# A pair's products with v in one run, in the banks of its scores, for the last two batches

## The chip, the cores and the metric

The program runs on one core of a Trainium2 chip. The metric is the device time of one execution in microseconds. On the core, TensorE multiplies matrices (PE in the profile; PEld is its loading of weights), VectorE (DVE), ScalarE (ACT) and GpSimd (POOL) work on tiles, and SyncE (SP) issues the DMAs. TensorE writes its results to PSUM, which has 8 banks of 512 float32 words in each of 128 partitions; the tiles that the engines read lie in SBUF.

## The reference

Causal attention with a decay (4 batches, 8 heads, 576 positions, 64 wide), then a gated feed-forward layer (512 to 1536 to 512), then a second feed-forward layer of 8 experts (1024 wide) that are mixed by a balanced gate. All is float32.

```python
scores = scale * np.matmul(q, k.transpose(0, 1, 3, 2))
decay = cum[:, :, :, None] - cum[:, :, None, :]
scores = np.where(causal, -1000000000.0, scores + decay)
attn = np.exp(scores - np.max(scores, axis=-1, keepdims=True))
attn = attn / (np.sum(attn, axis=-1, keepdims=True) + 1e-09)
out = np.matmul(attn, v)
...
g = x @ w_gate
x = (g * (1.0 / (1.0 + np.exp(-g))) * (x @ w_val)) @ w_out      # 2304 tokens
...
for e in range(8):
    out += P[:, e:e + 1] * (np.maximum(x @ w1[e], 0.0) @ w2[e])
```

## The kernel before, in words

The work is laid out in stages. Attention of batch 0 runs alone; attention of batches 1, 2 and 3 runs beside the first feed-forward layer of batches 0, 1 and 2; then comes that layer for batch 3, and after it the experts, which take most of the time. `merge` emits the steps of two streams (attention and feed-forward) in proportion to fixed costs, and a scheduler of the framework then sets the order of each engine's instructions from the dependences and its own estimate of times. Every engine works its own list strictly in order, so the list can be read from the program, and a wait holds up all that stands behind it.

Attention takes two heads (a pair, `hp`) at a time, four pairs per batch. The 576 queries of a head are four blocks of 128 (`qi` 0 to 3) and a last one of 64 (both heads' last blocks share one tile). Per pair the steps are: `load`; `front_a` (scores of blocks 0 and 1); `back_a` (their exponentials, tiles `np`, turned by TensorE into PSUM, `ps_t`, copied to `pts[0]`, and multiplied with v: `pv(hp, 0)`); `front_b` and `scores_end` (scores of the other blocks); `back_b` (the same for blocks 2, 3 and the last into `pts[1]`, then `pv(hp, 1)`); `fold` (the products, tile `bt`, times the reciprocals of the row sums, `rb`, and split into a high and a low part, `xh` and `xl`, which the feed-forward layer of that batch reads).

Scores go to `ps_s` (two banks, one tile at a time in these stages), turned blocks to `ps_t` (two tiles of a bank), products with v to `ps_o` (one bank, one tile), and the feed-forward layer has `ps_m` (three banks: `pm` for the products with w_gate and w_val, `py` for those with w_out, `pl` for the gate's logits). Nearly all matmuls use the whole array, 128 columns of weights. The products with v do not: a head's v is 64 wide, so each takes one half of the array's columns (128x64 weights), and the two heads of a pair are sent in turns (`e` 1, then 0). `pv(hp, 0)` has 2 blocks of keys and `pv(hp, 1)` has 5, so 4 and 10 matmuls; they are float32, and the profile counts each as two. `behind(one)` asks the scheduler to keep a run's matmuls together.

Batches 2 and 3 (`MASKED`) differ from 0 and 1: their scores come from split operands (`qkw`), and the decay and the mask (`cb`, `cm`, `cd`, loaded by DMA and added to on GpSimd) are added by VectorE in `step` and not by TensorE. The change touches these two batches only.

The reciprocals of a pair's row sums take a way of their own: ScalarE and VectorE make `rc`, TensorE turns it (`ps_r`), VectorE copies it (`rt`), a DMA writes it to DRAM (`rd`), four DMAs read it back spread over the partitions (`rb`).

Of the kernel before, what the change touches and what calls it, by code (L numbers as in the profile page):

```python
# [8 lines left out]
F32 = mybir.dt.float32  # L9
# [24 lines left out]
def attention_two_ffns(ctx: ExitStack, tc: tile.TileContext, qkT, vt, f, wf, g2, w1, w2, out):  # L34
    nc = tc.nc
# [5 lines left out]
    P = 128  # L41
# [23 lines left out]
    ident = const.tile([P, P], F32, name="ident")  # L65
# [13 lines left out]
    for rows, c in ((slice(0, 64), 0), (slice(64, P), 64)):  # L79
        nc.vector.tensor_copy(out=maskd[rows], in_=maskf[rows, rows])  # L80
        nc.vector.tensor_reduce(
            out=picks[rows], in_=ident[rows, c:c + 3 * NG].rearrange("p (n j) -> p n j", j=3),
# [65 lines left out]
    last_pv = [None]  # L148
# [5 lines left out]
    MASKED = (2, 3)  # L154
# [59 lines left out]
    for e in range(2):  # L214
        spread_in = nc.sync.dma_start(
            out=spread[64 * e:64 * e + 3 * NG],
            in_=cumt[16 * e:16 * e + NG].rearrange("n j s -> (n j) s"))

    WA, WB = 256, 320
# [7 lines left out]
    pts = [ptp.tile([P, n, 2, w], F32, name=f"pt{n}") for n, w in ((2, WA), (5, WB))]  # L227
# [2 lines left out]
        nc.vector.memset(vss[i][0:64, 4], 0.0)  # L230

    def attn_unit(b, ps_s, ps_t, ps_o):
        heads = {}

        def load(hp):
            if hp == 0:
# [42 lines left out]
        def behind(ins):  # L279
            hold = ExitStack()  # L280
            if ins is not None:
                hold.enter_context(tc.issue_after(ins.ins))
                hold.enter_context(tc.high_priority(offset=SOON))
            return hold
# [125 lines left out]
        def turn(pt, n, k0):  # L410
            ps = ps_t.tile([P, 512], F32, tag="t", name="ps_t")
            for j in range(n):
                c = k0 + j * P
                nc.tensor.transpose(ps[:, j * P:(j + 1) * P], pt[:, c:c + P], ident)  # L414
            return ps[:, 0:n * P]

        def trans(hp, qi, e):
            n = qi + 1
            ps = turn(heads[hp][-1].pop((qi, e)), n, 0)
            c = qi % 2 * P  # L420
            copy = nc.vector.tensor_copy if qi in ONV else nc.scalar.copy
            copy(out=pts[qi // 2][:, 0:n, e, c:c + P], in_=ps.rearrange("p (j q) -> p j q", j=n))

        def trans_end(hp):
            pt = heads[hp][-1].pop(4)
            ps = turn(pt, 4, 0)
            nc.vector.tensor_copy(
                out=pts[1][:, 0:4, :, 256:WB], in_=ps.rearrange("p (j e q) -> p j e q", j=4, e=2))
            ps = turn(pt, 1, 448)
            nc.scalar.copy(out=pts[1][:, 4, :, 256:WB], in_=ps.rearrange("p (e q) -> p e q", e=2))  # L430

        def pv(hp, rng):
            vs, bt = heads[hp][4:6]
            w, t0 = ((WA, 0), (WB, 256))[rng]
            po = ps_o.tile([P, 512], F32, tag="o", name="ps_o")
            one, n = None, (2, 5)[rng]
            for j in range(n):
                c0 = max(0, j * P - t0)
                for e in (1, 0):
                    rows = HALF[e]  # L440
                    with behind(one):
                        one = nc.tensor.matmul(  # L442
                            out=po[rows, c0:w], lhsT=vs[:, j, rows], rhs=pts[rng][:, j, e, c0:w],
                            start=(j == 0), stop=(j == n - 1))
            last_pv[0] = one
            nc.scalar.copy(out=bt[:, t0:t0 + w], in_=po[:, 0:w])

        def fold(hp):
            bt = heads[hp][5]
# [18 lines left out]

        def back_a(hp):
            for qi in range(2):  # L470
                for e in range(2):
                    trans(hp, qi, e)
            pv(hp, 0)

        def front_b(hp):
            scores(hp, 2)
# [2 lines left out]
        def back_b(hp):  # L479
            for qi in range(2, 4):  # L480
                for e in range(2):
                    trans(hp, qi, e)
            trans_end(hp)
            pv(hp, 1)

        return [(c, lambda fn=fn, hp=hp: fn(hp)) for hp in range(H // 2) for c, fn in
                ((0.6, load), (1.6, front_a), (1.4, back_a), (2.4, front_b), (1.6, scores_end), (4.0, back_b), (0.3, fold))]


# [101 lines left out]
    with ExitStack() as hold:  # L591
        room = banks(hold, 2, 3)
        idle = room[1].tile([P, 512], F32, tag="t", name="idle")
        for _ in range(WARM):
            nc.tensor.matmul(out=idle[:, 0:P], lhsT=ident, rhs=ident, start=True, stop=True)
        for n, (_, fn) in enumerate(attn_unit(0, *room)):
            fn()
            for i in LOADS.get(n, ()):
                sts[i] = wload0(i, spread_in if i == 1 else last_qk[0])
            if n in ROWS:  # L600
                rows.append(last_step[0])
            if n in TURNS:
                w0.append(convert(len(w0)))
# [8 lines left out]
    ps_m = m_ctx.enter_context(pool("ps_m", 3, space=PSUM, reuse_waits="tile"))  # L612
    room = banks(at_ctx, 1, 2)
    merge(attn_unit(1, *room), moe_unit(0, convert, w0), lead=LA)
    merge(attn_unit(2, *room), moe_unit(1), lead=LB)
    merge(attn_unit(3, *room), moe_unit(2), lead=LC)
    at_ctx.close()
# [303 lines left out]
```

## Time and profile before

| What | Value |
|---|---|
| median of 3 runs | 2212.11 us (2211.51 to 2214.68) |
| the profiled execution's own time | 2213.49 us |
| its span, from the first to the last instruction | 2211.7 us |
| PE busy | 2174.7 us, 98% of the span |
| DVE busy | 1603.3 us, 72% |
| ACT busy | 780.1 us, 35% |
| POOL busy | 837.0 us, 38% |

The granted clock of TensorE is a share of full speed: 1.00 is its level of 2.4 GHz and 0.50 that of 1.2 GHz; 0.996 is the mean over the span. In a timeline, a row is a group of like instructions that follow each other, with the start of the first, the time from there to the end of the last, and their count at the end; a bracket behind it tells how long the engine had been idle before and what it waited for. Matmuls overlap, so the time that a group costs is not its own length but the distance from its start to the start of the next group. Attention of batches 2 and 3 falls between about 240 and 511 us.

### The profile page before, as it was taken

Reading aid. Unit: us, or ns where it says so; the run is one execution under the profiler, and the core shown is the slowest. Engines: PE = TensorE matmul, PEld = TensorE weight load, DVE = VectorE, ACT = ScalarE, POOL = GpSimd, SP = SyncE. Lnnn points to the kernel's source line nnn. Section 1 sums busy time; section 2 is a strip of 40 time slices with the busy share of each in tenths; the row PEclk is TensorE's granted clock in tenths of the full one; section 3 lists DMA queues with packets and bytes.
Section 4 is the critical chain, followed back from the end, with each engine's and each line's share of the span. In section 5 each row is a group of like instructions: output and inputs, shape, how many; then the busy total and the mean of one; then the engine's idle time right before and its main releaser. Section 6 shows DMA issues by size and latency. Waiting matters only on the chain.

```text
span 2211.7 us, 35903 instructions
## 1 busy us (share of the span) xinstructions
PE 2174.7 (98%) x13861; PEld 1957.7 (89%) x13861; DVE 1603.3 (72%) x3285; ACT 780.1 (35%) x1837; POOL 837.0 (38%) x659
## 2 busy tenths in 40 slices
PE   8899999999999999999999999999999999999999
PEld 5778989989899898898888899999999999999997
DVE  8766534444345897888888887877888888888876
ACT  7655554452323342332332322333322322323221
POOL 5677544433334332433343432332322323323320
PEclk9999999999999999999999999999999999999999
DMA  7766675646442111222122211341111111111111
GB/s 217 278 214 215 202 204 162 204 137 215 173 170 72 49 49 39 89 72 71 47 98 66 69 48 39 132 157 39 50 47 39 58 39 39 58 39 44 52 29 53
DMA packets 105515, 225.25 MB, mean 102 GB/s; under 512 B 9748, under 2 KB 63296, under 8 KB 93696
## 3 DMA queue, kind: packets, MB, share of 16 engines
q1 hardware_dynamic: 105344, 222.95, 30.8%
q8 instruction: 109, 1.79, 0.3%
q14 instruction: 62, 0.51, 0.1%
HBM read 185.96 MB, written 36.96 MB: 101 GB/s over the span
## 4 chain that ended last, share of the span: by engine, by line
PE 87%; DVE 4%; DMA 4%; ACT 1%; POOL 1%; issue 1%; SPq 1%; POOLq 0%; DVEq 0%; ACTq 0%
PE py L172 41%; PE pa L756 32%; PE pm L172 10%; DMA st<-wf 2%; PE ps_o L442 2%; DMA xst<-xd 1%; PE ps_t L414 1%; PE ps_s L318 1%; DVE g L127 1%; DVE np L288 1%; DMA rd<-rt 1%; DVE st L130 1%; DVE g L124 1%; DMA rb<-rd 1%; DMA cd<-cumd 0%
## 5 line engine op out<-in xcount | busy, mean ns | idle before, releaser
L756 PE MATMUL pa<-xf,w1h 128*128 128x288 f32 x3584 | 741.7, 294 | 0.0
L756 PEld LDWEIGHTS pa<-xf,w1h 128*128 128x128 f32 x3584 | 597.3, 188 | 36.3
L809 DVE SCALAR_TENSOR_TENSOR acc<-py,lg,acc 128x512 f32<-128x512 f32 x531 | 394.8, 744 | 236.8 <-PE py L172 236.3
L756 PE MATMUL pa<-xf,w1l 128*128 128x288 f32 x1792 | 527.9, 295 | 0.0
L172 PE MATMUL py<-w2l,ah 128*128 128x512 f32 x1152 | 453.5, 394 | 0.0
L172 PE MATMUL py<-w2h,ah 128*128 128x512 f32 x1152 | 452.9, 393 | 0.1
L172 PE MATMUL py<-w2h,al 128*128 128x512 f32 x1152 | 450.5, 391 | 0.0
L164 POOL TENSOR_TENSOR w2l<-w,w2h 128x1024 fp32r<-128x1024 f32 (+1 forms) x72 | 156.5, 2179 | 758.8 <-ACT w2h L731 757.9
L771 DVE SCALAR_TENSOR_TENSOR al<-c,ah 128x288 fp32r<-128x288 f32 x512 | 422.2, 853 | 6.6 <-ACT ah L770 6.1
L770 ACT ACTIVATE ah<-c 128x288 fp32r<-128x288 f32 x512 | 208.3, 443 | 558.4 <-PE py L172 310.1
L756 PEld LDWEIGHTS pa<-xf,w1l 128*128 128x128 f32 x1792 | 336.7, 188 | 10.2
L172 PE MATMUL pm<-xh,w 128*128 128x288 f32 x1536 | 325.2, 298 | 5.6 <-DVE th L524 1.7
L172 PEld LDWEIGHTS pm<-xh,w 128*128 128x128 f32 x1536 | 251.8, 189 | 12.4 <-DVE xa L542 3.0
L172 PEld LDWEIGHTS py<-w2h,al 128*128 128x128 f32 x1152 | 216.4, 188 | 48.4
L172 PEld LDWEIGHTS py<-w2h,ah 128*128 128x128 f32 x1152 | 216.2, 188 | 28.8 <-DVE acc L809 2.0
L172 PEld LDWEIGHTS py<-w2l,ah 128*128 128x128 f32 x1152 | 216.3, 188 | 24.5
L164 POOL TENSOR_TENSOR w1l<-w,w1h 128x256 fp32r<-128x256 f32 x192 | 160.4, 863 | 184.3 <-ACT w1h L727 176.1
L172 PE MATMUL pm<-xl,w 128*128 128x288 f32 x768 | 226.7, 295 | 0.5 <-POOL xl L164 0.5
L777 ACT COPY m<-pa 128x288 f32<-128x288 f32 x128 | 50.4, 394 | 378.6 <-PE pa L756 378.2
L172 PE MATMUL py<-ah,w 128*128 128x288 f32 x768 | 171.7, 301 | 4.8 <-DVE th L524 2.3
L164 POOL TENSOR_TENSOR w1l<-sm,w1h 128x1024 fp32r<-128x1024 f32 (+1 forms) x72 | 157.3, 2190 | 4.7 <-ACT w1h L727 4.7
L164 POOL TENSOR_TENSOR al<-th,ah 128x288 fp32r<-128x288 f32 x96 | 84.1, 876 | 192.6 <-ACT ah L526 187.6
(159 smaller groups left out, 2684.0 us busy)
## 6 DMA issues: line engine op xcount, KB each, us to landing
w<-w SPq DMA_DIRECT2D x128, 512.0 KB
w<-wsplit SPq DMA_DIRECT2D x54, 1024.0 KB
st<-wf SPq DMA_DIRECT2D x19, 1024.0 KB
wsplit<-w SPq DMA_DIRECT2D x18, 1024.0 KB
qk<-qkT SPq DMA_DIRECT2D x48, 288.0 KB
xo<-h SPq DMA_DIRECT2D x28, 288.0 KB
xf<-xo SPq DMA_DIRECT2D x14, 576.0 KB
xd<-xa SPq DMA_DIRECT2D x8, 576.0 KB
```

The source lines that it names most:

```text
L124: nc.vector.tensor_scalar(out=g, in0=top, scalar1=0x7fff, scalar2=None, op0=ALU.bitwise_and)
L127: nc.vector.scalar_tensor_tensor(out=g, in0=top, scalar=0x8000, in1=g, op0=ALU.bitwise_and, op1=ALU.bitwise_or)
L130: nc.vector.scalar_tensor_tensor(out=v, in0=mid, scalar=2.0**-36, in1=y.bitcast(BF16), op0=ALU.mult, op1=ALU.mult)
L164: (eng or nc.gpsimd).tensor_tensor(out=out, in0=src, in1=hi.bitcast(F32), op=ALU.subtract)
L172: ins = nc.tensor.matmul(out=ps, lhsT=a, rhs=b, start=(i == 0), stop=(i == n - 1))
L288: last_step[0] = nc.vector.tensor_tensor_reduce(out=out, in0=src, in1=add, scale=-SCALE, scalar=prev, op0=ALU.add, op1=ALU.min, accum_out=m)
L442: one = nc.tensor.matmul(out=po[rows, c0:w], lhsT=vs[:, j, rows], rhs=pts[rng][:, j, e, c0:w], start=(j == 0), stop=(j == n - 1))
L756: last_pa[0] = nc.tensor.matmul(out=ps, lhsT=w[:, MW[m - 1], k], rhs=x[:, m - 1, hl, k], start=(n == 0), stop=(n == len(ops) - 1))
L770: nc.scalar.activation(out=ah[:, f, tk], in_=src, func=AF.Relu)
L771: nc.vector.scalar_tensor_tensor(out=al[:, f, tk], in0=src, scalar=0.0, in1=ah[:, f, tk].bitcast(F32), op0=ALU.max, op1=ALU.subtract)
L777: nc.scalar.copy(out=m1, in_=p1)
L809: nc.vector.scalar_tensor_tensor(out=a, in0=py, scalar=lg[:, t, e:e + 1], in1=a, op0=ALU.mult, op1=ALU.add)
```

## The change

For batches 2 and 3 the products of the first two blocks are no longer formed in `back_a`. `back_b` forms them right behind those of the other blocks, into the two banks of one tile from the pool of the scores (`ps_s`, still called `ps_o`), and two copies on ScalarE bring them to `bt` at the end. The transposes of a first block go for both heads into one bank and are copied by one instruction (`trans_both`), two copies a pair where there were four. `trans_end` turns the small piece first.

```diff
+        def trans_both(hp, qi):
+            n, c = qi + 1, qi * P
+            ps = ps_t.tile([P, 512], F32, tag="t", name="ps_t")
+            for e in range(2):
+                pt = heads[hp][-1].pop((qi, e))
+                for j in range(n):
+                    k = (e * n + j) * P
+                    nc.tensor.transpose(ps[:, k:k + P], pt[:, j * P:(j + 1) * P], ident)
+            nc.scalar.copy(out=pts[0][:, 0:n, :, c:c + P].rearrange("p j e q -> p e j q"),
+                           in_=ps[:, 0:2 * n * P].rearrange("p (e j q) -> p e j q", e=2, j=n))
...
         def trans_end(hp):
             pt = heads[hp][-1].pop(4)
...
+            if b in MASKED:
+                ps = turn(pt, 1, 448)
+                nc.scalar.copy(out=pts[1][:, 4, :, 256:WB], in_=ps.rearrange("p (e q) -> p e q", e=2))
+                ps = turn(pt, 4, 0)
+                nc.vector.tensor_copy(
+                    out=pts[1][:, 0:4, :, 256:WB], in_=ps.rearrange("p (j e q) -> p j e q", j=4, e=2))
...
         def pv(hp, rng):
...
-            po = ps_o.tile([P, 512], F32, tag="o", name="ps_o")
             one, n = None, (2, 5)[rng]
+            if b not in MASKED:
+                po = ps_o.tile([P, 512], F32, tag="o", name="ps_o")
+            else:
+                if rng:
+                    pos[0] = ps_s.tile([P, 2, 512], F32, tag="s", name="ps_o")
+                else:
+                    one = last_pv[0]
+                po = pos[0][:, rng]
...
             last_pv[0] = one
-            nc.scalar.copy(out=bt[:, t0:t0 + w], in_=po[:, 0:w])
+            if b not in MASKED:
+                nc.scalar.copy(out=bt[:, t0:t0 + w], in_=po[:, 0:w])
...
         def back_a(hp):
             for qi in range(2):
-                for e in range(2):
-                    trans(hp, qi, e)
-            pv(hp, 0)
+                if b in MASKED:
+                    trans_both(hp, qi)
+                else:
+                    for e in range(2):
+                        trans(hp, qi, e)
+            if b not in MASKED:
+                pv(hp, 0)
...
             trans_end(hp)
             pv(hp, 1)
+            if b in MASKED:
+                pv(hp, 0)
+                for t0, w, i in ((256, WB, 1), (0, WA, 0)):
+                    nc.scalar.copy(out=heads[hp][5][:, t0:t0 + w], in_=pos[0][:, i, 0:w])
```

The first place is on PE, the second run of the last pair of batch 2 before the change; `pt_197` is `pts[0]`, `pt_198` is `pts[1]`, `vs_200` holds v.

```order
1353 L414 MATMUL ps_t<-ident,np 128x128
1354 L442 MATMUL ps_o<-pt_198,vs_200 64x320 x6
1355 L442 MATMUL ps_o<-pt_198,vs_200 64x192 x2
1356 L172 MATMUL pm<-xh,w 128x288
1357 L172 MATMUL pm<-xl,w 128x288
1358 L172 MATMUL pm<-xh,w 128x288 x2
1359 L172 MATMUL pm<-xl,w 128x288
1360 L172 MATMUL pm<-xh,w 128x288 x2
1361 L172 MATMUL pm<-xl,w 128x288
1362 L172 MATMUL pm<-xh,w 128x288
1363 L442 MATMUL ps_o<-pt_198,vs_200 64x64 x2
1364 L172 MATMUL pm<-xh,w 128x288
```

The same engine with the change, a pair of batch 2:

```order
1500 L172 MATMUL py<-al,w 128x288
1501 L172 MATMUL py<-ah,w 128x288
1502 L467 MATMUL ps_o<-pt_198,vs_200 64x320 x6
1503 L467 MATMUL ps_o<-pt_198,vs_200 64x192 x2
1504 L467 MATMUL ps_o<-pt_198,vs_200 64x64 x2
1505 L467 MATMUL ps_o<-pt_197,vs_200 64x256 x2
1506 L467 MATMUL ps_o<-pt_197,vs_200 64x128 x2
1507 L172 MATMUL pm<-xh,w 128x288
```

The 14 products with v of a pair stand in one run. Before, the 4 of the first blocks stood elsewhere, and here the 10 others were in two pieces. In all, the 8 pairs of batches 2 and 3 have 20 such pieces before (16 runs, 4 of them broken once: three by feed-forward matmuls, one by a `ps_r`), and 8 now.

The second place is on POOL, the end of attention. Before the change (`al` is work of the feed-forward layer, `w1l` and `w2l` that on the first weights of the experts, `xst` and `xf` the loading of batch 0 for them, `f` the input of the gate's logits):

```order
176 L164 TENSOR_TENSOR w1l<-w_8202,w1h 128x2x128 x3
177 L164 TENSOR_TENSOR w1l<-sm,w1h 128x2x2x128 x2
178 L164 TENSOR_TENSOR w2l<-w_8204,w2h 128x512 x2
179 L164 TENSOR_TENSOR al<-th,ah 128x288 x2
180 L460 TENSOR_TENSOR bt<-bt,rb 128x576
181 L164 TENSOR_TENSOR al<-th,ah 128x288
182 L164 TENSOR_TENSOR xl<-bt,xh 128x2x288
183 L164 TENSOR_TENSOR al<-th,ah 128x288 x9
184 L164 TENSOR_TENSOR xf<-xst,xf 128x2x288
```

With the change:

```order
174 L164 TENSOR_TENSOR w1l<-w_8162,w1h 128x2x128 x3
175 L164 TENSOR_TENSOR w2l<-w_8164,w2h 128x512 x2
176 L164 TENSOR_TENSOR w1l<-sm,w1h 128x2x2x128 x2
177 L486 TENSOR_TENSOR bt<-bt,rb 128x576
178 L164 TENSOR_TENSOR al<-th,ah 128x288 x2
179 L164 TENSOR_TENSOR xl<-bt,xh 128x2x288
180 L164 TENSOR_TENSOR al<-th,ah 128x288 x2
181 L164 TENSOR_TENSOR f<-xa,f 128x576
182 L164 TENSOR_TENSOR xf<-xst,xf 128x2x288
183 L164 TENSOR_TENSOR xf<-xst,xf 128x288
184 L164 TENSOR_TENSOR f<-xa,f 128x576
```

The last pair's `bt` and `xl` have moved nearer to the end of the feed-forward layer of batch 2: 9 `al` stood between `xl` and `xf`, and now 2. On PE, 470 matmuls stood between the last product with v and the first one that reads `xh` of batch 3, and now 145.

## Rows read from the trace of the kernel before

**Rows 1.** The page's first part: busy us (share of the span) xinstructions of each engine.
```profile
PE 2174.7 (98%) x13861; PEld 1957.7 (89%) x13861; DVE 1603.3 (72%) x3285; ACT 780.1 (35%) x1837; POOL 837.0 (38%) x659
```

**Rows 2.** Windows by stage: us, busy PE, PEld, DVE, ACT, POOL; clock, DMA, GB/s.
```profile
240.00:300.00 60.00, 56.87 (x419) 50.67 (x418) 27.62 (x105) 35.04 (x97) 35.59 (x31) 0.97 0.79 218
300.00:511.00 211.00, 208.48 (x1595) 196.63 (x1594) 93.42 (x312) 98.22 (x258) 88.72 (x82) 1.00 0.57 178
```

**Rows 3.** Timeline of PE, an unbroken second run (start, length, what, count).
```profile
503.22 0.29 PE L172 MATMUL pm<-xh,w 128*128 128x288 f32 x1
503.44 2.28 PE L442 MATMUL ps_o<-pt,vs 128*64 128x320 f32 x20
...
505.88 0.29 PE L172 MATMUL pm<-xl,w 128*128 128x288 f32 x1
```

**Rows 4.** Timeline of PE, a second run in two pieces.
```profile
350.10 0.27 PE L414 MATMUL ps_t<-ident,np 128*128 128x128 f32 x1
350.30 2.16 PE L442 MATMUL ps_o<-pt,vs 128*64 128x320 f32 x16
352.39 0.40 PE L172 MATMUL pm<-xh,w 128*128 128x288 f32 x1
352.63 0.29 PE L172 MATMUL pm<-xl,w 128*128 128x288 f32 x1
...
353.55 0.29 PE L172 MATMUL pm<-xh,w 128*128 128x288 f32 x1
353.77 0.34 PE L442 MATMUL ps_o<-pt,vs 128*64 128x64 f32 x4
...
354.27 0.29 PE L172 MATMUL pm<-xl,w 128*128 128x288 f32 x1
```

**Rows 5.** Timeline of PE, transposes between whole-array matmuls.
```profile
346.12 0.29 PE L172 MATMUL py<-al,w 128*128 128x288 f32 x1
346.25 0.29 PE L172 MATMUL py<-ah,w 128*128 128x288 f32 x1
346.38 1.03 PE L414 MATMUL ps_t<-ident,np 128*128 128x128 f32 x8
347.17 0.36 PE L318 MATMUL ps_s<-qkw 128*128 128x256 f32 x1
```

**Rows 6.** Lines of ACT, 300 to 511 us: line, shapes, count, busy, mean ns, idle before.
```profile
L446 ACT COPY bt<-ps_o 128x320 f32<-128x320 f32 x6 | 2.6, 428 | 10.0 <-PE ps_o L442 9.9
L446 ACT COPY bt<-ps_o 128x256 f32<-128x256 f32 x5 | 1.9, 373 | 3.3 <-PE ps_o L442 3.3
```

**Rows 7.** Timelines of POOL and PE, the longest stall between 240 and 300 us.
```profile
292.57 0.32 POOL L270 TENSOR_TENSOR cd<-cd,zmaskd 128x64 f32<-128x64 f32 x1 [8.81 <-DMA cd<-cumd]
...
294.62 0.40 PE L172 MATMUL py<-ah,w 128*128 128x288 f32 x1 [1.63 <-DVE th L524]
```

**Rows 8.** Window behind that stall.
```profile
295.00:300.00 5.00, 5.00 (x29) 4.98 (x28) 2.82 (x12) 3.87 (x11) 3.51 (x4) 0.66 0.50 179
```

**Rows 9.** Timelines at the last pair's end: PE, POOL.
```profile
508.91 0.27 PE L398 MATMUL ps_r<-ident,rc 128*9 128x128 f32 x1
...
506.57 2.15 POOL L164 TENSOR_TENSOR w1l<-w,w1h 128x256 fp32r<-128x256 f32 x3 [2.73 <-DMA w<-w]
...
511.19 2.54 POOL L164 TENSOR_TENSOR w2l<-w,w2h 128x512 fp32r<-128x512 f32 x2
...
519.05 1.43 POOL L460 TENSOR_TENSOR bt<-bt,rb 128x576 f32<-128x576 f32 x1 [3.22 <-DMA rb<-rd]
...
521.27 1.43 POOL L164 TENSOR_TENSOR xl<-bt,xh 128x576 fp32r<-128x576 f32 x1
```

**Rows 10.** Timeline of PE where the feed-forward layer of batch 3 begins.
```profile
567.35 0.40 PE L172 MATMUL py<-ah,w 128*128 128x288 f32 x1 [0.50 <-DVE xa L542]
...
569.70 0.31 PE L557 MATMUL pl<-f,gw 128*16 128x288 f32 x1 [1.30 <-ACT f L553]
...
574.64 0.56 PE L557 MATMUL pl<-f,gw 128*16 128x288 f32 x3 [0.66 <-POOL f L164]
```

More of the change, by code (lines that the diff above doesn't have):

```diff
@@ L232, in attn_unit @@
     def attn_unit(b, ps_s, ps_t, ps_o):
-        heads = {}
+        heads, pos = {}, [None]
         def load(hp):
@@ L425, in trans_end @@
             pt = heads[hp][-1].pop(4)
[L426 to L430, printed above, removed]
+            if b in MASKED:
[5 more added lines that the diff above has]
+            else:
+                ps = turn(pt, 4, 0)
+                nc.vector.tensor_copy(
+                    out=pts[1][:, 0:4, :, 256:WB], in_=ps.rearrange("p (j e q) -> p j e q", j=4, e=2))
+                ps = turn(pt, 1, 448)
+                nc.scalar.copy(out=pts[1][:, 4, :, 256:WB], in_=ps.rearrange("p (e q) -> p e q", e=2))
         def pv(hp, rng):
@@ L470, in back_a @@
             for qi in range(2):
-                for e in range(2):
-                    trans(hp, qi, e)
-            pv(hp, 0)
+                if b in MASKED:
+                    trans_both(hp, qi)
+                else:
+                    for e in range(2):
+                        trans(hp, qi, e)
+            if b not in MASKED:
+                pv(hp, 0)
         def front_b(hp):
```

## The prediction

> **What bounds the kernel now.** I read the page's busy times, then the windows by stage, then timelines of TensorE inside the stage that the change touches. The first is to show that TensorE is busy in 98% of the span and nothing else above 72% [rows 1]. That share can hide idle stretches in one stage, so the windows come next: from 300 to 511 us, where attention of batches 2 and 3 runs beside the feed-forward layer, TensorE is busy in 208.48 of 211 us at a granted clock of 1.00 (2.4 GHz), and ScalarE, VectorE and GpSimd in less than half [rows 2]. So in this stage time is what TensorE's list of matmuls costs, plus 2.5 us of idling; from 240 to 300 us there are 3.1 us of idling and a clock of 0.97. What other engines save is worth nothing unless TensorE waits for them. The timelines then tell what a matmul costs by its neighbours, which busy time doesn't.
>
> **The products in one run.** The number of matmuls and their columns stay the same. What changes is how often TensorE goes from products that use all 128 columns of weights to the half-array products with v (128x64) and back. Feed-forward matmuls follow each other every 0.13 us (346.12, 346.25, 346.38 [rows 5]). An unbroken second run: from 503.22 to 505.88 there are 2.66 us, of which two feed-forward matmuls take 0.26, so the run costs 2.40 [rows 3]. The same run in two pieces: from 350.10 to 352.63 there are 2.53 us, less 0.13 for a `pm` and 0.10 for a transpose (eight take 0.79 us [rows 5]), which leaves 2.30; from 353.55 to 354.27 there are 0.72 us, less 0.26, which leaves 0.46 [rows 4]. Together 2.76, so 0.36 more for one break, with the same columns sent. The small piece says it again: 4 times 64 columns at 288 columns per 0.13 us (the pace of `pm`) would take 0.12, and cost 0.46, an excess of 0.34. I take 0.35 us per excursion to the half array, half before and half behind it: the matmul behind it starts 0.24 us before its successor where 0.13 is usual (352.39 to 352.63).
>
> The program has 20 such pieces in batches 2 and 3 before and 8 with the change, as the lists of TensorE's instructions show. 12 times 0.35 is 4.2 us. One of the 12 is a break by a single `ps_r`, a matmul with 9 columns of weights, which may cost less; without it the sum is 3.85. I take 4.2. As the stage is bound by TensorE, all of it is on the path.
>
> **The merged transposes.** Their number is unchanged, and runs of transposes carry no surcharge against whole-array products: eight take 0.79 us and the next one starts on time [rows 5]. So one bank for two heads is worth nothing on TensorE. ScalarE has 16 copies fewer, but is busy in 98 of 211 us [rows 2]; nothing, as the idle time hides it. The new order in `trans_end` moves a small copy ahead; nothing, hidden by the feed-forward matmuls between the transposes and the run.
>
> **What moves.** The copies of the products wait for the whole run, about 0.80 us of ScalarE a pair (428 and 373 ns [rows 6]). They now hold the bank pair of the scores, so the next pair's first scores wait for them. Behind those scores on TensorE stands feed-forward work, and behind that everything. Of the seven runs with a pair behind them, three have 36 whole-array matmuls (4.7 us) and two have 24 (3.2 us) between the run and those scores, by the list of TensorE's instructions, which covers it; the other two (one for each batch) have 7 and 3 logit matmuls (0.9 and 0.4 us), not enough, and about half a microsecond may be lost in each. Likewise the run must wait for the copies of the last turned blocks; in the same two places only 0.6 us stand between. That is up to 2 us in all. Against it stand the idle stretches of before, which need not come again: attention now reaches further into the stage (a pair starts later and loads later), so the DMAs spread. The longest stall: GpSimd waited 8.81 us for a `cd` load, the feed-forward work queued behind it was late, TensorE idled 1.63 us [rows 7], and the window behind it shows a granted clock of 0.66, the level of 1.2 GHz in part of it, which is 1.7 us of 5 [rows 8]. Together the idling and the clock are worth 3.1 + 2.5 + 1.7 = 7.3 us between 240 and 511 [rows 2, 8]. The ends are that all of it goes, or that it doubles; the nearest value is that as much remains, and I take nothing.
>
> **The end of attention.** The last pair now ends 145 matmuls (19.1 us) ahead of the first that reads `xh` of batch 3. Two chains must fit. From `ps_r` to the end of `xl` before were 508.91 to 522.70, 13.8 us [rows 9]; now the 18 `py`, the run and the 145 behind it stand in between, 24 us. And GpSimd does 7.2 us on the experts' first weights (506.57 to 513.73), then `bt` 1.43, two `al` 1.6 (one is what lies between `bt` and `xl`, 0.8), `xl` 1.43 [rows 9], about 13 us behind the run with its copies. Both fit, by 6 us at least, so I cost it at nothing. On SP, the load `xst` waits for that `xl` and now stands behind one more weight load: about 3 us later against the feed-forward matmuls than before. The `f` that the logits need now stands behind `xf`, which waits for `xst`. But that place already costs: 0.50, 1.30 and 0.66 us of idling [rows 10]. It may fall to nothing or double, 2.5 us either way; I take nothing. Behind it the lists are the same apart from such shifts.
>
> Sum: 2213.49 of the profiled execution less 4.2 is 2209.3; that execution is 1.38 above the median, so 2212.11 less 4.2, **2207.9 us**, for the median. About 0.2% (4.4 us) is what a measurement of this kernel can tell from no change, so this forecast lies on that edge.
>
> **The rivals.**
> - *The stall goes too.* The DMAs come in another order and `cd` is not late. Then 1.63 + 1.7 [rows 7, 8] come on top: 2212.1 - 4.2 - 3.3 = 2204.6. For it: the load was issued into a stretch in which the DMA engines were busy 0.79 of the time [rows 2]. Against it: that stretch still has three weight loads ahead of the pair's.
> - *The gain is eaten by new waits.* A scores bank that is held longer, and runs right behind their last transposes, idle TensorE by some 0.4 us a pair, plus a little at the logits: 3 to 4 us, 2211.5. For it: attention has one pair of score banks, and now three uses for it. Against it: the 24 or 36 matmuls behind most runs.
> - *The bank must be emptied first.* Every pair pays the copies, 0.80 [rows 6] and about as much until they begin: 8 times 1.6 is 12.8, less 4.2, if nothing covered them; with cover behind two runs of three about 0 net, 2212. The Trainium skill (TensorEngine Tiling (Array Packing), Performance Considerations) says that packing the array speeds up TensorE but not the emptying of PSUM, which may become the bottleneck. The rows show ScalarE idle before these copies, 10.0 us before six [rows 6], so here the copies wait for TensorE and not the other way.
> - *Slower: the last pair comes too late.* `rb` of the last pair is read behind weight loads; if `xl` ends 15 us later than worked out (the point from which it decides is 6), TensorE idles 9 us at the first product of batch 3: 2217. For it: 470 matmuls of cover before, 145 now. Against it: the whole chain took 13.8 us before [rows 9].
> - That the scheduler pulls the runs apart again is excluded by the list of instructions: all 8 are whole.
>
> **How the numbers follow.** The forecast 0.39, the stall goes too 0.26, eaten by new waits 0.23, emptied first 0.04, the last pair too late 0.08. The forecast's own spread is 2 us to both sides, so half of it falls under 2207.7. Faster by over 0.2%: 0.26 + 0.20 = 0.46. Within: 0.19 + 0.23 + 0.04 = 0.46. Slower: 0.08. The range goes from 2202.5, where two thirds of the 7.3 us go as well less what the logits may add, to 2214, where they grow by 6; that leaves out the slower rival and the far ends.
>
> **What would show it.** In the profile after: 8 runs of 28 half matmuls, each with one slow start and one slow successor; TensorE's busy time in 240 to 511 us less by about 4; the same idle sum there. The forecast is wrong if TensorE waits for `bt` copies (`ps_s` behind ScalarE), if `pm` of batch 3 waits for `xl`, or if the logits wait longer for `f`. If the time falls and the runs are whole but an excursion costs other than 0.35, the term is mis-sized.

## The result, and the profile after

The changed kernel took 2226.57 us (median of 6 runs, 2225.91 to 2236.35) against 2214.31 us (2211.51 to 2216.08) of the kernel before on the same chips: ratio 1.0067, 95% interval 1.0055 to 1.0078. That is 12 us slower by the medians (15 by the ratio, on which the one run of 2236.35 us weighs); the forecast was 2207.9 with a range to 2214. The span of the profiled execution grew by 14.5 us.

TensorE's share of the whole span is as before, and again hides the stage (the page's busy times, then the windows of [rows 2]):

```profile
PE 2177.9 (98%) x13861; PEld 1960.3 (88%) x13861; DVE 1604.9 (72%) x3285; ACT 777.7 (35%) x1821; POOL 836.0 (38%) x659
```

```profile
240.00:300.00 60.00, 56.48 (x420) 50.51 (x420) 23.13 (x79) 29.82 (x74) 32.67 (x27) 0.97 0.71 210
300.00:511.00 211.00, 199.45 (x1486) 189.34 (x1485) 85.72 (x295) 88.71 (x231) 84.73 (x79) 0.98 0.57 171
```

From 240 to 511 us TensorE idles 3.5 + 11.6 = 15.1 us, where it idled 5.7 [rows 2], and the granted clock in the long window is 0.98 where it was 1.00. Idling brings 9.4 us, the clock some 4 (0.02 of 211; the figure is rounded), the products' saving takes 4.2 off. That is 9 of the 14.5. Another 1.5 us of idling lies between 130 and 240 us (busy 102.71 of 110 us before, 101.16 after). Up to about 239 us the lists of all five engines are the same in both kernels, so I don't put it down to the change. Some 4 us I can't itemise.

The runs themselves came out as forecast. TensorE's timeline after, one of the eight:

```profile
469.84 0.30 PE L172 MATMUL pm<-xh,w 128*128 128x288 f32 x1
470.07 2.93 PE L467 MATMUL ps_o<-pt,vs 128*64 128x320 f32 x28
472.92 0.40 PE L172 MATMUL pm<-xh,w 128*128 128x288 f32 x1
473.16 0.29 PE L172 MATMUL pm<-xl,w 128*128 128x288 f32 x1
```

and a first run of the kernel before:

```profile
413.50 0.29 PE L172 MATMUL pm<-xh,w 128*128 128x288 f32 x1
413.71 0.87 PE L442 MATMUL ps_o<-pt,vs 128*64 128x256 f32 x8
414.51 0.40 PE L172 MATMUL pm<-xh,w 128*128 128x288 f32 x1
414.75 0.29 PE L172 MATMUL pm<-xl,w 128*128 128x288 f32 x1
```

Joined: 473.16 - 469.84 less two `pm` at 0.13 is 3.06 us. Apart: 2.40 [rows 3] and 1.25 - 0.26 = 0.99, together 3.39. So 0.33 saved for one excursion, where 0.35 was taken. Added up in this way over all 20 pieces and 8 runs (each distance from start to start, less the usual one of its kind), the surcharge is 6.1 us before and about 2.4 after: 3.7 us saved, 0.31 an excursion.

**Where the time went.** TensorE's longest stall after (timelines of PE, POOL, ACT and SP):

```profile
361.14 0.61 PE L172 MATMUL py<-ah,w 128*128 128x288 f32 x1 [3.91 <-DVE th L558]
...
347.31 0.81 POOL L164 TENSOR_TENSOR al<-th,ah 128x288 fp32r<-128x288 f32 x1
358.12 1.40 POOL L486 TENSOR_TENSOR bt<-bt,rb 128x576 f32<-128x576 f32 x1 [9.99 <-DMA rb<-rd]
...
359.55 0.67 ACT L488 CAST xh<-bt 128x576 fp32r<-128x576 f32 x1 [6.44 <-POOL bt L486]
360.12 0.40 ACT L557 ACTIVATE th<-pm 128x288 f32<-128x288 f32 x1
...
338.49 1.33 SPq L243 DMA_DIRECT2D qk<-qkT  x2
339.92 0.54 SPq L159 DMA_DIRECT2D w<-wsplit  x1
340.56 0.29 SPq L402 DMA_DIRECT2D rd<-rt  x1
...
351.12 0.46 SPq L406 DMA_DIRECT2D rb<-rd  x1
```

Read from the bottom: the reciprocals leave at 340.56, right behind the next pair's loads and a 1 MB weight load, and the first load that reads them back is issued 10.6 us later. GpSimd waits for it until 358.12, ScalarE's `xh` for GpSimd until 359.55. A tanh that has all that it needs stands behind `xh` on ScalarE; TensorE needs what comes of it. Before the change, the same way for a pair was (SP):

```profile
346.63 0.33 SPq L159 DMA_DIRECT2D w<-wsplit  x1
...
358.31 0.29 SPq L402 DMA_DIRECT2D rd<-rt  x1
359.58 0.46 SPq L406 DMA_DIRECT2D rb<-rd  x1
```

There the read-back is issued 1.3 us behind `rd`. The difference is in what the DMA engines still had to do (windows behind `rd`, before and after; the last two figures are their busy share, where about 1 is full, and GB/s):

```profile
358.30:359.60 1.30, 1.30 (x12) 1.30 (x11) 0.45 (x1) 0.22 (x2) 0.00 (x0) 1.00 0.07 13
340.00:351.00 11.00, 11.00 (x92) 9.89 (x92) 4.15 (x15) 3.21 (x10) 1.27 (x3) 1.00 1.04 274
```

The stall of 2.66 us that ends at 308.37 is of the same kind; there the copies of `py` stand behind `xh` (ACT, PE):

```profile
307.02 0.67 ACT L488 CAST xh<-bt 128x576 fp32r<-128x576 f32 x1 [4.51 <-POOL bt L486]
307.59 0.43 ACT L560 CAST ah<-th 128x288 fp32r<-128x288 f32 x1
307.93 0.69 ACT L574 COPY xa<-py 128x288 f32<-128x288 f32 x2
...
308.37 0.40 PE L172 MATMUL py<-ah,w 128*128 128x288 f32 x1 [2.66 <-ACT xa L574]
```

The second kind of stall (SP, ACT, DVE, PE):

```profile
439.41 0.46 SPq L406 DMA_DIRECT2D rb<-rd  x1
439.96 0.57 SPq L596 DMA_DIRECT2D lgd<-ls  x1
...
442.44 0.41 ACT L557 ACTIVATE th<-pm 128x288 f32<-128x288 f32 x1 [4.19 <-DMA lgd<-ls]
...
442.89 0.46 DVE L558 SCALAR_TENSOR_TENSOR th<-th,pm 128x288 f32<-128x288 f32 x1 [5.29 <-ACT th L557]
...
443.39 0.40 PE L172 MATMUL py<-ah,w 128*128 128x288 f32 x1 [2.20 <-DVE th L558]
```

`ls`, the copy of the gate's logits, uses one of the two buffers of `th`. Its store to DRAM stands on SP behind a load of `rb` that waits for the reciprocals. A tanh on ScalarE waits for the buffer.

A third kind comes from the order on GpSimd (POOL, PE):

```profile
252.97 5.94 POOL L164 TENSOR_TENSOR qkw<-qk,qkw 64x576 fp32r<-64x576 f32 x4
258.86 1.40 POOL L164 TENSOR_TENSOR xl<-bt,xh 128x576 fp32r<-128x576 f32 x1
...
260.31 0.40 PE L172 MATMUL pm<-xl,w 128*128 128x288 f32 x1 [1.94 <-POOL xl L164]
```

The `xl` of batch 1 stands on GpSimd behind four splits of the next pair's operands. Before the change one such split stood between its `bt` and it, and TensorE did not wait there.

The sums of the first two kinds over 236 to 620 us (ScalarE's waits), before (first fence) and after (second), from the view of waits: us in total, times, longest.

```profile
ACT xh L462 <- POOL bt L460: 12.7, 6, 3.7
...
ACT th L523 <- DMA lgd<-ls: 0.9, 1, 0.9
```

```profile
ACT xh L488 <- POOL bt L486: 24.1, 9, 6.4
...
ACT th L557 <- DMA lgd<-ls: 7.8, 3, 4.2
```

13.6 us of waiting before, 31.9 after. TensorE's own waits after, 240 to 511 us, show the kinds above in their first three rows. What the prediction had feared is small (the rows for `ps_s` and the logits):

```profile
PE py L172 <- DVE th L558: 6.7, 3, 3.9
PE py L172 <- ACT xa L574: 5.0, 3, 2.7
PE pm L172 <- POOL xl L164: 1.9, 1, 1.9
...
PE ps_s L318 <- ACT bt L518: 0.3, 1, 0.3
...
PE pl L591 <- POOL f L164: 0.2, 1, 0.2
```

### The profile page after: what moved, and what is told of

Same layout as the page of the kernel before. It is cut to its first block, busy times and chain, and to the rows that moved or that the text cites. A ratio compares the mean times of both kernels' runs of the same rounds, so it can differ in the third digit from the quotient of the medians.

```text
span 2226.2 us, 35862 instructions
## 1 busy us (share of the span) xinstructions
PE 2177.9 (98%) x13861; PEld 1960.3 (88%) x13861; DVE 1604.9 (72%) x3285; ACT 777.7 (35%) x1821; POOL 836.0 (38%) x659
## 4 chain that ended last, share of the span: by engine, by line
PE 84%; DMA 6%; DVE 4%; POOL 2%; ACT 1%; SPq 1%; issue 1%; POOLq 0%; ACTq 0%; DVEq 0%
PE py L172 39%; PE pa L790 31%; PE pm L172 9%; DMA st<-wf 2%; DMA rd<-rt 1%; PE ps_o L467 1%; DMA rb<-rd 1%; PE ps_t L414 1%; DMA xst<-xd 1%; PE ps_s L318 1%; DMA w<-wsplit 1%; POOL qkw L164 1%; DVE g L124 0%; DMA xo<-h 0%; POOL bt L486 0%
## 5 line engine op out<-in xcount | busy, mean ns | idle before, releaser
L790 PEld LDWEIGHTS pa<-xf,w1l 128*128 128x128 f32 x1792 | 336.7, 188 | 10.2
L558 DVE SCALAR_TENSOR_TENSOR th<-th,pm 128x288 f32<-128x288 f32 x96 | 43.3, 452 | 166.3 <-ACT th L557 166.2
```

What stands on the lines that cost most here:

```text
L558: nc.vector.scalar_tensor_tensor(out=th, in0=th, scalar=1.0, in1=pg, op0=ALU.add, op1=ALU.mult)
L790: last_pa[0] = nc.tensor.matmul(out=ps, lhsT=w[:, MW[m - 1], k], rhs=x[:, m - 1, hl, k], start=(n == 0), stop=(n == len(ops) - 1))
```

## The experiments

Two later cures are short. *The hold*: the scaling of a pair's products (`bt`, `xh`, `xl`) is queued behind the latest feed-forward instructions that were written when the next pair's first scores were.

```diff
+            with ExitStack() as hold:
+                if b in MASKED and hp < H // 2 - 1:
+                    for i in last_a:
+                        hold.enter_context(tc.issue_after(i.ins))
+                nc.gpsimd.tensor_tensor(out=bt, in0=bt, in1=rb, op=ALU.mult)
...
+                steps += [(0.6, load, hp), (1.6, front_a, hp)]
+                if hp:
+                    steps.append((0.2, fold, hp - 1))
```

(`last_a` holds the last `ah` cast and the last `al`; the reciprocals leave at the end of `back_b` as before.) *The buffer* (for all batches):

```diff
-            ls = tmp.tile([P, HB], F32, tag="th", name="ls")
+            ls = tmp.tile([P, HB], F32, tag="ls", name="ls")
```

In the table, the two columns of waits are ScalarE's of the view above: `xh` for GpSimd's `bt`, and `th` for the store of the logits. "Run" says where the products go that are written as one run; without a word they are written as two. "Pieces" are those into which TensorE's trace shows the products of the 8 pairs divided, 8 where all runs are whole. The ratio is to the runs of the kernel before on the same chip, whose median was 2213.4 to 2214.3 each time.

| Label | run | pieces | new turning | hold | buffer | us | ratio (95%) | xh | th |
|---|---|---|---|---|---|---|---|---|---|
| before | | 20 | | | | 2214 | 1 | 12.7 | 0.9 |
| changed | scores' banks | 8 | yes | | | 2226.57 | 1.0067 (1.0055 to 1.0078) | 24.1 | 7.8 |
| turn_only | | 16 | yes | | | 2224.17 | 1.0049 (1.0035 to 1.0062) | 31.6 | 3.4 |
| run_only | scores' banks | 12 | | | | 2228.84 | 1.0068 (1.0056 to 1.0080) | 25.4 | 11.9 |
| own_banks | own | 10 | yes | | | 2220.18 | 1.0026 (1.0017 to 1.0035) | 26.0 | 5.9 |
| no_trip | scores' banks | 8 | yes | | | 2220.23 | 1.0027 (1.0016 to 1.0037) | 8.0 | 4.3 |
| small_first | | 16 | its order alone | | | 2221.75 | 1.0036 (1.0024 to 1.0048) | 22.9 | 5.4 |
| before_held | | 22 | | yes | | 2206.92 | 0.9975 (0.9965 to 0.9986) | 8.2 | 0.5 |
| held_lead | | 21 | | yes | | 2207.95 | 0.9974 (0.9965 to 0.9983) | 13.8 | 0.6 |
| held_small | | 16 | its order alone | yes | | 2208.61 | 0.9979 (0.9970 to 0.9988) | 12.2 | 3.1 |
| held_turn | | 16 | yes | yes | | 2216.03 | 1.0012 (1.0001 to 1.0023) | 12.3 | 6.5 |
| held_run | own | 12 | | yes | | 2207.84 | 0.9976 (0.9967 to 0.9984) | 4.9 | 2.6 |
| own_held | own | 10 | yes | yes | | 2214.00 | 1.0003 (0.9994 to 1.0013) | 14.5 | 10.2 |
| after_held | scores' banks | 8 | yes | yes | | 2218.81 | 1.0026 (1.0017 to 1.0035) | 10.0 | 13.0 |
| after_ls | scores' banks | 8 | yes | | yes | 2220.15 | 1.0032 (1.0020 to 1.0043) | 36.3 | 0 |
| held_run_ls | own | 13 | | yes | yes | 2207.36 | 0.9973 (0.9964 to 0.9983) | 11.2 | 0 |
| own_held_ls | own | 8 | yes | yes | yes | 2204.26 | 0.9960 (0.9946 to 0.9974) | 10.6 | 0 |
| after_held_ls | scores' banks | 8 | yes | yes | yes | 2201.43 | 0.9946 (0.9934 to 0.9959) | 10.6 | 0 |
| before_held_ls | | 21 | | yes | yes | 2204.45 | 0.9954 (0.9941 to 0.9968) | 18.8 | 0 |
| after_held_ls_lead | scores' banks | 8 | yes | yes | yes | 2203.42 | 0.9949 (0.9937 to 0.9962) | 8.1 | 0 |

**First: parts of the change.**

turn_only (`pv` and the copies to `bt` as before):

> The kernel before with only the turned blocks changed: the first blocks of both heads turned into one bank and copied at once, the small piece of the last block first; the products with v stay in 20 pieces. Theory 1 (in the changed kernel the reciprocals' way through DRAM comes late, and ScalarE, GpSimd and SyncE, which work in order, hold feed-forward work behind it): within 2 us of before, 2214. Theory 2 (the scores' bank pair is held by the products, so that a pair cannot begin before the last one is copied out): 2214 as well. Theory 3 (no place of the chip's, only another order, which any edit can bring): off by 4 us or more to either side.

run_only (`trans_both` and the order in `trans_end` taken back):

> The changed kernel without the joint turning and with the large piece of the last block first, as before; the products in one run in the scores' banks. Theory 1 and theory 2: slow like the changed kernel, 2223 to 2229, since the run and its banks are what moves the reciprocals. Theory 3: anything between 2208 and 2230.

own_banks:

```diff
-                    pos[0] = ps_s.tile([P, 2, 512], F32, tag="s", name="ps_o")
+                    po = ps_o.tile([P, 512], F32, tag="o", name="ps_o")
...
+                    po = ps_t.tile([P, 512], F32, tag="t", name="ps_o")
```

> The changed kernel with the run's products in the bank that they had (ps_o) and one of the two of the turned blocks (ps_t) in place of the scores' two banks. Theory 2: the scores' banks are free again, TensorE's idling of 20 us between 240 and 690 us falls by 9 and the two half-speed stretches go, 2209 to 2213. Theory 1: the reciprocals of a pair still leave beside the next pair's loads, 2221 to 2228. Theory 3: anything.

no_trip:

```diff
+                    nc.sync.dma_start(out=rb[rows, 0:512], in_=cumd[r:r + 1, 0:512].to_broadcast([64, 512]))
+                    nc.sync.dma_start(out=rb[rows, 512:S], in_=cumd[r:r + 1, 512:S].to_broadcast([64, 64]))
```

> The changed kernel, where the four loads of rb for batches 2 and 3 read a row of the decays in DRAM of the same size and not the reciprocals that were just written, so that they wait for nothing of the pair (the products of these batches are then scaled with other numbers; everything else is computed as before). Theory 1: GpSimd's wait for rb (41.9 us) and ScalarE's behind it (24.1 us) nearly go, TensorE's idling falls by 6 to 9 us and the clock's loss by 3 to 5: 2211 to 2217. Theory 2: still 2224 to 2228. Theory 3: anything.

None of the three theories came out clean. The turning alone costs 10 us, which theories 1 and 2 exclude; 2.7 us of it are TensorE's waits for the joint copies of `pt`, since in turn_only the products of the first blocks follow them at once. Nor are the parts clean: turn_only has 16 pieces and not 20, as the second runs are whole with the small piece first, and without that order 4 of the 8 runs of run_only come apart. Own banks win 6 us back and the reciprocals' way 6 us by the medians (9 by the ratios), each about half. In the stage itself no_trip recovered more than its median shows:

```profile
300.00:511.00 211.00, 206.39 (x1580) 195.99 (x1579) 89.80 (x306) 92.92 (x240) 87.51 (x81) 1.00 0.58 176
```

4.6 us of idling at a clock of 1.00, against 11.6 at 0.98. From 0 to 130 us it was busy 2.3 us less than the changed kernel (112.52 and 114.80), although the lists of all engines are the same in both up to about 255 us: two executions of the same work can differ by that much, and one profile of a stage tells no finer.

**Second: the hold, and an edit that costs nothing.**

> The kernel before; in batches 2 and 3 the scaling of a pair's products (bt times rb on GpSimd, xh on ScalarE, xl) is queued behind the latest feed-forward work that was written when the next pair's first scores were, some 5 us later, so that an unfinished load of rb holds up less. Theory 1 (the late reciprocals): GpSimd's wait for rb falls from 24.3 us to under 10, 2208 to 2213, a few us for a kernel that suffers little from it. Theory 3 (any edit reorders, and the order of the kernel before is a lucky one): 2218 to 2226, as the four other edits gave.

> The changed kernel with the same hold. Theory 1: GpSimd's wait for rb falls from 41.9 us to under 15 and TensorE's time with it, 2212 to 2219. Theory 2 (the held scores' banks): 2224 to 2229. Theory 3: anything from 2215 to 2230.

> The products in one run in banks of their own, with the same hold. If theories 1 and 2 each carry a part (own banks were worth 6 us and the waiting reciprocals 6 us against the changed kernel) and add up: 2212 to 2216. If both remove the same stalls: 2218 to 2221. Theory 3: anything.

small_first (the new order of `trans_end` in the kernel before, and nothing else):

> The kernel before with one edit alone that costs or saves nothing on any engine: in batches 2 and 3 the small piece of the last block is turned and copied ahead of the large one. Theories 1 and 2: within 2 us of 2214. Theory 3: it reorders like the others, 2218 to 2226.

small_first lost 8 us for swapping two small pieces of work, although it closed all four breaks of the second runs (16 pieces): theory 3 is right that the order decides, and the kernel before has a good one (of the six without a cure it alone is under 2220). Theory 1 is right that late reciprocals cost in each of the three orders tried: the hold won 6.5, 7.8 and 6.2 us, and made the kernel before faster, its stage full:

```profile
300.00:511.00 211.00, 211.00 (x1614) 198.76 (x1613) 96.61 (x317) 96.40 (x257) 85.31 (x80) 1.00 0.58 180
```

But because it won about the same in all three, it didn't explain the 12 us between the changed kernel and before.

**Third: parts again, with the hold.**

> The kernel before with the hold on the scaling (2206.9 by itself), and the small piece of the last block first. Theory 3 (a neutral edit moves the order of the queues, and with it a few stalls): if the hold takes away the queue positions by which the order hurts, 2205 to 2210; if not, 2212 to 2218, the 8 us of the small piece alone again. Theory 1 (late reciprocals alone): 2205 to 2209.

> The same with the whole new turning (both heads' first blocks in one bank, copied at once, and the small piece first), products in two pieces as before. Theory 3: 2212 to 2220 as far as the hold doesn't help; theory 1: 2205 to 2209. A cost of the joint turning itself (the copy waits for both heads) would show as TensorE waiting for the copies of pt: 2210 or more here with held_small at 2207.

> The same hold, the turning as before, and the products in one run in banks of their own (ps_o and one of ps_t). If the run is a gain by itself once the stalls are gone: 2202 to 2205, 4.2 less than 2206.9. If the run itself brings stalls (its bank of ps_t keeps the next turned blocks waiting, and the copies come at once): 2211 to 2216, with TensorE waiting for bt or pt at ps_t. Theory 3: anything from 2203 to 2216.

held_lead (LB, LC 1.1 in place of 1.2):

> The kernel before with the hold, and with attention of batches 2 and 3 emitted at a lead of 1.1 in place of 1.2; no work is changed, only where in the feed-forward work it falls. Theory 3: 2 to 10 us more than 2206.9. Theories 1 and 2: within 2 us of it.

With the hold, another lead and the small piece first cost 1 to 2 us only, and the run in own banks 1; but with the large piece first that run was not whole (12 pieces). held_turn lay 9 us above before_held, where theory 3 or a cost of the joint turning had put it. Its trace showed a wait that is longer in all kernels above 2215 us so far than in the kernel before (ACT, then PE):

```profile
283.15 0.42 ACT L567 CAST ah<-th 128x288 fp32r<-128x288 f32 x1
290.06 0.41 ACT L564 ACTIVATE th<-pm 128x288 f32<-128x288 f32 x1 [6.49 <-DMA lgd<-ls]
...
291.01 0.61 PE L172 MATMUL py<-ah,w 128*128 128x288 f32 x1 [3.03 <-DVE th L565]
```

The largest stall there comes from the store of the logits (the bracket of `th`), not from the turning. The turning has a smaller one:

```profile
385.81 0.87 PE L462 MATMUL ps_o<-pt,vs 128*64 128x256 f32 x8 [1.48 <-ACT pt L427]
```

Over 13 of the 14 kernels up to here a line through time against ScalarE's two waits added has a slope of 0.70 us per us and a correlation of 0.94. That gave theory 4. The one left out is no_trip, slow at 12.3 us of waits; with it the slope is 0.62 and the correlation 0.86.

**Fourth: the logits' buffer.**

> The changed kernel, where the logits' copy ls has a buffer of its own and no longer one of the two of th, so that no tanh on ScalarE waits for the store of the logits to DRAM (7.8 us of ScalarE's waiting in the changed kernel). Theory 4 (ScalarE works in order and waits for two ways through DRAM, for the reciprocals before xh and for the logits' store before a th; over the 13 kernels so far 0.70 us of time for each us of these two waits, on top of 2201): 2219 to 2223, since the 24.1 us before xh remain. Theory 3 (the order as such): 2222 to 2231, no fall.

> The changed kernel with both cures, the hold on the scaling and the buffer for ls. Theory 4: ScalarE's 13.0 us for the logits' store go, 2207 to 2212. Theory 2 (the scores' banks held by the products): 2215 to 2220, with TensorE waiting at ps_s for the copies to bt. Theory 3: 2214 to 2224.

> Products in one run in banks of their own and the new turning, with both cures. Theory 4: 10.2 us of waiting go, 2205 to 2209. Theory 3: 2211 to 2219. If the joint turning costs by itself: 2211 or more while ScalarE no longer waits.

> Products in one run in banks of their own, turning as in the kernel before, with both cures. Theory 4: 2.6 us of waiting go, 2204 to 2207, the fastest so far if the run's 4.2 us are real; theory 3: 2206 to 2214.

The wait for the store was gone in all four. What the buffer took off goes with what had been waited: 13.0 us waited, 17.4 won (after_held); 10.2, 9.7 (own_held); 7.8, 6.4 (changed); 2.6, 0.5 (held_run; too little to tell from nothing). In after_ls the wait for `xh` grew to 36.3 us and the time fell all the same. after_held_ls beats both kernels, and lies 5.6 us below theory 4's range. Theory 2 falls as the main cause: this kernel keeps the products in the scores' banks and is 3 us faster than own_held_ls (with the hold alone, after_held was 5 us slower than own_held). Its waits and windows, where TensorE idles 2.0 + 0.4 us (the 2.0 are the stall on `xl` of batch 1 again, which no cure touches):

```profile
ACT xh L499 <- POOL bt L497: 10.6, 4, 6.2
```

```profile
240.00:300.00 60.00, 57.97 (x441) 53.12 (x441) 22.95 (x78) 31.34 (x78) 32.90 (x28) 0.97 0.70 207
300.00:511.00 211.00, 210.58 (x1627) 202.44 (x1627) 94.36 (x311) 92.40 (x237) 88.09 (x82) 1.00 0.61 190
```

**Fifth: the change's own worth.**

> The kernel before with both cures, to take the change's own worth from a pair in which ScalarE's two waits are small on both sides: after_held_ls had 2201.4. Theory 4 with the saving of the prediction (12 excursions at 0.35): 2204.5 to 2207, that is 3 to 6 us above it. If the cures alone made after_held_ls fast and the run is worth nothing: 2200 to 2203.

> The changed kernel with both cures and attention at a lead of 1.1 in place of 1.2, another order for the same work. Theory 4: 2200 to 2206, as the waits stay away in another order as well. Theory 3 (2201.4 is the luck of one order): 2208 or more.

Another lead keeps the time within 2 us, so 2201.4 is not the luck of that one order (a third was not tried). Without the cures the changed kernel is 12 us slower than the kernel before, with both it is not slower: the loss lies in what the two cures take away. With both, the change is 3.0 us faster by the medians, 0.0008 (1.8 us) by the ratios, whose intervals overlap: in the direction of the forecast, and not told from nothing by these times. held_run_ls, the run in own banks with the old turning, points the other way: 2.9 us slower than before_held_ls by the medians, though with 13 pieces against 21; one stall of 2.0 us at `ps_t` stands in its trace. So the run's worth in time stays open. before_held_ls also breaks theory 4's line: 18.8 us of ScalarE's waiting for `xh` and no loss; all six kernels with the buffer lie below that line, by 1 to 10 us. A wait costs only where what stands behind it has no slack; for `xh` that depends on the place. Each cure reorders the lists too, so no single pair is a proof; five pairs for the buffer (the fifth, before_held, 0.5 waited and 2.5 won) and six for the hold (6.2 to 18.7 won) all point one way. How much of a gain is the shorter wait and how much the new order, these runs don't separate.

## Why the prediction was wrong

The step that failed is "the ends are that all of it goes, or that it doubles; the nearest value is that as much remains, and I take nothing", on idling and clock between 240 and 511 us. It was set at the 7.3 us of before and came out near 21: 15.1 of idling, and some 6 by the clock (0.03 of 60 us and 0.02 of 211). Even its upper end, twice 7.3, was too low. In its place the runs showed feed-forward work held up behind `xh` and the logits' store on ScalarE (13.6 us of waits before, 31.9 after), and no loss once both were eased.

- *Why it failed.* It followed one stall (`cd`, [rows 7]) and reasoned that attention reaching further would spread the DMAs. It didn't list what else stands in order on ScalarE, GpSimd and SP. Before, SP issued `rd` of one pair at 358.31, 11 us behind the next pair's `qk` loads, with the DMA engines nearly idle; after, at 340.56, directly behind them. The waits of before (GpSimd 24.3 us for `rb`, ScalarE 12.7 for `xh`) stood in its trace and were not priced as something that an order can double.
- *The products in one run*: right on TensorE's list in kind and size, 8 whole runs, 0.33 against 0.35 where feed-forward matmuls stand on both sides, 3.7 us against 4.2 in all. That the time falls by it is not shown.
- *The merged transposes and the small piece first, nothing*: right for the busy times, wrong for the kernel. Where the products follow at once TensorE waits for the joint copy (2.7 us in turn_only, 1.5 in held_turn), and small_first alone moved the time by 8 us. Nor is the small piece first nothing for the pieces: it accounts for 4 of the 12 (16 pieces in small_first), and without it runs come apart (12 in run_only).
- *What moves, the scores' banks and the copies, 0 to 2 us*: right, 0.3 us. The rival that priced them (gain eaten by new waits) looked for the wait at the wrong engine.
- *The end of attention, nothing*: right. `xl` of the last pair ended at 576.1 where it was 522.70 [rows 9], its run of products also later (560.38 where it was 503.44), and TensorE has no wait for it behind 511 us; the slower rival, with 0.08, did not happen. Nor did the stall go (308.37 and 361.14 took its place), and ScalarE's copies did not bind.
- *What would show it*: of the signs named for a wrong forecast none appeared beyond the 0.3 us for `bt`. What failed, "the same idle sum", was in the list of what should hold. Of the same list, TensorE's busy time in 240 to 511 us fell by 9.4 us and not by 4, but it says nothing of the saving: TensorE did 1906 matmuls there and not 2014.
- *The range*: its lower end doesn't follow from its words. Two thirds of 7.3 are 4.9, so 2207.9 less 4.9 is 2203.0, and less what the logits may add it lies above that, not at 2202.5. Nothing hung on it.

## What to carry to other kernels

Where a scheduler sets the order, price an edit by the slack of every in-order queue that it can shuffle, not only by what it adds: here an edit that adds no work moved the time by 8 us. Look for a way through DRAM in the list of an engine on the path (a scaling that waits for a read-back, a buffer shared with something that is being stored), and give it a buffer of its own or a place further back first; before that a gain of this size can't be looked for. Read from the engine's list or trace whether each variant is what its name says: here five variants of "one run" had runs in two or three pieces. Compare a change in two or three orders before saying what it is worth.

## What was not expected of the hardware

The granted clock fell to 0.50, the level of 1.2 GHz, at three of TensorE's stalls after: right behind 1.94 us (to 260.31) and 2.66 us (to 308.37), and within 3.91 us (to 361.14):

```profile
262.00:264.00 2.00, 2.00 (x10) 0.86 (x8) 0.00 (x0) 0.00 (x0) 1.73 (x2) 0.50 0.85 187
309.00:312.00 3.00, 3.00 (x14) 3.00 (x14) 0.00 (x0) 1.47 (x6) 0.93 (x2) 0.50 0.31 52
360.00:366.00 6.00, 4.86 (x20) 4.84 (x21) 3.55 (x14) 2.86 (x8) 2.48 (x3) 0.50 0.00 0
366.00:372.00 6.00, 6.00 (x43) 5.83 (x42) 3.43 (x12) 2.00 (x5) 1.74 (x2) 0.94 0.59 188
```

Behind the 2.20 us of 443.39 it stayed at 1.00 (window 440 to 460 us), while before it had fallen behind 1.63 [rows 7, 8]. In these traces the length of a stall alone doesn't tell whether the clock falls. So a stall of the changed kernel cost up to twice what its idling shows: 3.91 us, and some 3 more while the feed-forward matmuls came every 0.24 us (361.55 to 361.79) in place of 0.13.
